# Attention with a routed expert layer on one core: pair numbers of four blocks in their own tiles, later batches' loads and clears between fetches, last stores on SyncE's queue

## The chip, the cores and the metric

The kernel runs on one core of a Trainium2 chip. The metric is the device time of one execution in microseconds (us); the median of several runs counts. The engines are named as the profile names them: PE is the matrix engine, PEld its weight loads, DVE, ACT and POOL the vector, scalar and GpSimd engines, SP the engine whose queue issues most DMAs. Each engine works its instructions off in the order in which they were emitted.

## The reference, cut to what matters

```python
a = einsum('rd,bhsd->bhsr', S1, x); b = einsum('rd,bhsd->bhsr', S2, x)
phi(x) = einsum('bhsi,bhsj->bhsij', a, b).reshape(..., r * r)        # r = 8: 64 features
num = phi(q) @ (phi(k)^T v);  den = phi(q) @ sum_s phi(k) + 1e-06    # per batch and head
x = (num / den) -> (4352, 128)                                       # B=4, H=4, S=1088, head_dim 32
noisy = x @ w_gate + log1p(exp(x @ w_noise)) * noise                 # 8 experts
top2, weights = the two largest of noisy, softmax over the two
out[n] = sum over n's two experts e of weight * (relu(x[n] @ w1[e]) @ w2[e])   # 128 -> 1024 -> 128
```

Everything is fp32. In one sentence: a linear attention over 4 batches makes 4352 token rows of 128, each row goes to two of eight experts (a two-layer network with 1024 hidden units), and the two results are added.

## The kernel before, in words

The four batches' attention and the experts' blocks are interleaved in one instruction stream. The program is not written out by hand: class `Plan` (from L38) collects jobs (`add`), each with the engines that may do it, an estimated cost, what it reads and writes, a priority and the tiles it opens. `order()` then plays the jobs through a simple model of the engines, and of those that could start first (within 0.3 us) takes the one with the lowest priority number. The emitted order on each engine is the planned one, so what the model believes of a transfer's landing decides where the work that needs it is put. A job's `margin` is added to its believed landing. All transfers go through `dma` (L338 is the issuing line), which takes the queue's engine, the priority and the margin. `later(u, ...)` marks loads that are held until the fetch of block u has been issued ("rows u").

The stages, with their lines:

- **Loads.** `load_kq` brings k or q of one batch (544 KB) into a tile `kq` (two buffers), `load_v` brings v in six transfers into `vld` (one buffer), `load_w` brings w1 and w2 of one expert (512 KB each). `clear` writes zeros from the tile `pad` over rows of the DRAM buffer `xs` (516 KB each) ahead of its use.
- **Attention of a batch.** `keys_values`: DVE transposes k and q into kT and qT (L588, L590), PE multiplies them with S1 and S2 (L606), ACT or DVE copies, DVE forms the 64 features per head (L614, L628: `phk`, `phq`), PE sums keys times values (L669) and folds in the gates (L690). `queries`: PE transposes the features (L717), multiplies (L728), DVE divides (L743 to L747, L735).
- **Router.** `router`: a chain of DVE steps (L842 to L999) with counts on PE (L934, L937). It weighs the rows (`xg`, L986), and POOL scatters them by indirect DMAs to `xs` in DRAM (L809, 18 per batch, a spacer memset at L808 before each). A row in `xs` has 129 words: the 128 values and the pair number, which says where its result belongs.
- **Blocks.** Rows of one expert are taken in blocks u = 0 to 47, block u being expert u mod 8 of wave u div 8. Wave 0 holds the first four tiles of batch 0, wave 1 the rest of batch 0, waves 2, 3 and 4 batches 1, 2 and 3; the sixth wave holds what is left over. Blocks of waves 2 to 4 have 256 rows, the others 128. Blocks 0 to 3 are gathered on PE. Blocks 4 to 7 (below `QUICK`) are fetched on POOL's queue, whole rows with their pair numbers, into a tile `xb`, and PE transposes them (L1070). From block 8 on, SP issues four small fetches per block into `xb` (32 KB each) and one for the pair numbers into a tile `ix`, and DVE transposes (`bT`, L1084). `xb` has five buffers and `ix` five. Then come `hp` (L1094, PE), relu (L1102, ACT or L1100, DVE), `acc` (L1109, PE), the copy `y` (L322), and POOL's scatter of the results to the DRAM buffer `pairs` (L809), which reads the pair numbers: out of `xb` for blocks 4 to 7, out of `ix` from block 8 on. The last two blocks (46 and 47) are turned to tokens by a matmul instead (L1241).
- **Sums.** `sums` loads the two results of each token (`pr`), adds them on DVE (L1165; at the end also the matmul's part, L1172) and stores them. The three stores of the very last call are issued on the queues ("ACT", "POOL", "ACT"): 128 rows, 64 rows, 128 rows. Then every engine reads a flag (L1422), a branch follows (L1424) that is not taken unless an expert overflows, and the end barrier (L1452).

What sets the order around the change: SP's queue is one list. Fetches have the priorities −10 + u; k, q and v of batches 2 and 3 have 80 + 100 b and more and wait for "rows 8" and "rows 16". Of the rows of `xs`, clears 4 to 8 wait for the fetches of block 4 to 7 (`DIRECT`) with priorities 64 to 68. An instruction on SP that has to wait for a free buffer holds back all that stands behind it.

Of the kernel before, what the change touches and what calls it, by code (L numbers as in the profile page):

```python
# [174 lines left out]
def kernel(  # L175
# [15 lines left out]
    P = nc.NUM_PARTITIONS  # L191
    B, H, S, DH = q.shape
    R = S1.shape[0]
    D = H * DH
# [38 lines left out]
    def add(engines, cost, emit, **kw):  # L233

        if hold and engines in ("DVE", "PE"):
            kw["after"] = tuple(kw.get("after", ())) + tuple(hold)
        elif hold and engines == EV:
            engines = "ACT"
        return plan.add(engines, cost, emit, **kw)
# [3 lines left out]
    def tag(name, bufs, shape, dtype=F32, space=pool):  # L243
        plan.tag(name, bufs, lambda: space.tile(list(shape), dtype, name=name, tag=name, bufs=bufs))
# [34 lines left out]
    tag("mk", 1, [P, C + 1, E], BF16)  # L279
    tag("lim", 1, [P, E])  # L280
    tag("xb", 5, [P, 2, XW])
    tag("ix", 5, [P, 2])
    tag("bT", 3, [P, 2 * P])
    tag("h", 4, [P, 512])
    tag("y", 10, [P, 2 * D])
# [7 lines left out]
    def vec(n):  # L293
        return 0.155 + 0.00104 * n
# [13 lines left out]
    TABLE = 1.28  # L308
    ROWS = 1.0
    KLATE, VLATE, QLATE = 1.6, 1.3, 1.8  # L310
    MARGIN = 3.0
    LAND = 2.2
    def either(n):
        return {"ACT": act(n), "DVE": vec(n)}
# [715 lines left out]
    def block(u, w, e, r, n):  # L1030

        p0 = 1000 + 100 * u
        bT = new("bT")
        if u < QUICK:
            turn = new("turn")
        if u < DIRECT:
            oh = new("o")
            for c in range(4):
                add(("POOL" if u == 0 and c == 3 else "DVE"), 0.85 if u == 0 and c == 3 else vec(64), lambda e_, c=c: (
                    G if e_ == "POOL" else V).tensor_scalar(  # L1040
                    out=oh.t[:, c, :], in0=place[:], scalar1=onehot["pos"].t[:, c, e:e + 1],
                    scalar2=onehot["gm"].t[:, c, e:e + 1], op0=ALU.is_equal, op1=ALU.mult),
                    r=["place", onehot["pos"], onehot["gm"]], w=[(oh, c)], prio=-900 if u == 0 else 12.5 + u)

            for c in range(4):
                gather = add("PE", mm(P), lambda _, c=c: T.matmul(  # L1046
                    turn.t[:, 0:P], lhsT=onehot["x"].t[:, c, :], rhs=oh.t[:, c, :], start=(c == 0), stop=(c == 3)),
                    lat=0.15, r=[(oh, c), onehot["x"]], w=[turn], prio=p0 - 88)
            while behind_first:
                behind_first.pop().deps.add(gather)  # L1050
            xb = ix = first_rows
        else:
            xb, ix = new("xb"), new("ix")

            def done(ins):
                for w2 in range(w + 1, NW):
                    apart(ins, "scatter%d" % w2)
                behind(ins, *("scatter%d" % w2 for w2 in (w - 1, w)))
                wrote(ins, "fetch", "rows %d" % (u if u >= QUICK else DIRECT))
            there = routed.get(w, []) + routed.get(w - 1, [])  # L1060
            rows = xs_e[e, r:r + P * n, :]
            if u < QUICK:
                fetch = dma("POOL", lambda: xb.t[:, 0:n, :], lambda: rows.rearrange("(c p) x -> p c x", p=P),
                            there, [xb], -10 + u, size=66e3 * n, issue=0.55, done=done)
                for job in held[DIRECT]:
                    job.deps.add(fetch)

                def turns(_):
                    for c in range(n):
                        T.transpose(turn.t[:, P * c:P * c + P], xb.t[:, c, 0:D], ident[:])  # L1070
                add("PE", n * 0.14, turns, lat=0.15, r=[xb, "ident"], w=[turn], prio=p0 - 88)
            else:

                def flat():
                    return xb.t[:].rearrange("p c x -> p (c x)")[:, 0:P * n]
                for l in range(4):
                    fetch = dma("SP", lambda l=l: flat()[32 * l:32 * l + 32, :].rearrange("p (g x) -> p g x", x=32),
                        lambda l=l: rows[:, 32 * l:32 * l + 32].rearrange("(g p) x -> p g x", p=32),
                        there, [(xb, l)], -10 + u, size=16e3 * n, issue=0.5, done=done)
                    for job in held.get(u, ()):  # L1080
                        job.deps.add(fetch)
                dma("SP", lambda: ix.t[:, 0:n].unsqueeze(2), lambda: rows[:, D:XW].rearrange("(c p) x -> p c x", p=P),
                    there, [ix], -10 + u, size=0, issue=0.5, done=done)
                add("DVE", vec(P * n), lambda _: V.transpose(bT.t[:, 0:P * n], flat()), r=[xb], w=[bT], prio=TOP + u)  # L1084
        if u < QUICK:
            add(EV, either(P * n), lambda en: copy(en, bT.t[:, 0:P * n], turn.t[:, 0:P * n]), r=[turn], w=[bT], prio=TOP + u)
        acc = new("acc")
        js = 4 // n
        for g in range(FJ // js):
            hp, h = new("hp"), new("h")  # L1090

            def first(_, g=g, hp=hp):
                for i in range(js):
                    T.matmul(hp.t[:, P * n * i:P * n * (i + 1)], lhsT=w1s[:, e, P * (js * g + i):P * (js * g + i + 1)],  # L1094
                             rhs=bT.t[:, 0:P * n], start=True, stop=True)
            add("PE", js * mm(P * n), first, lat=0.15, r=[bT, ("w1", e)], w=[hp], prio=p0 + 10 * g)

            def relu(en, hp=hp, h=h):
                if en == "DVE":
                    paces.append(V.tensor_scalar_max(h.t[:], hp.t[:], 0.0))  # L1100
                else:
                    paces.append(A.activation(out=h.t[:], in_=hp.t[:], func=AF.Relu))  # L1102
            add(EV, either(512), relu, r=[hp], w=[h], prio=TOP + u)

            def second(_, g=g, h=h):
                for i in range(js):
                    for c in range(n):
                        j = js * g + i
                        T.matmul(acc.t[:, D * c:D * c + D], lhsT=h.t[:, P * (n * i + c):P * (n * i + c + 1)],  # L1109
                                 rhs=w2s[:, e, j, :], start=(j == 0 and c == 0), stop=(j == FJ - 1), skip_group_check=True)  # L1110
            add("PE", 4 * mm(D), second, lat=0.15, r=[h, ("w2", e)], w=[acc], prio=p0 + 10 * g + 15)
        y = new("y")
        add(EV, either(D * n), lambda en: copy(en, y.t[:, 0:D * n], acc.t[:, 0:D * n]), r=[acc], w=[y], prio=TOP + u)
        if w == NW and e >= E - LAST:
            to_tokens(e, ix, y, p0 + 98)
            return
        for c in range(n):
            def emit(_, c=c):
                at = first_at[:, e:e + 1] if u < DIRECT else xb.t[:, c, D:XW] if u < QUICK else ix.t[:, c:c + 1]
                ins = pool_scatter("result", out=pairs[:], in_=y.t[:, D * c:D * c + D], in_offset=None,  # L1120
                                   out_offset=bass.IndirectOffsetOnAxis(ap=at.bitcast(U32), axis=0),
                                   bounds_check=PAIRS - 1, oob_is_err=False)
                apart(ins, "result", "read")
                (behind if w >= NW - 1 else apart)(ins, "zero")
                wrote(ins, "result", "result%d" % w)
            key = ("result", (u, c))
            gone = add("POOL", ROWS + 0.3, emit, r=[y, xb if u < QUICK else ix] + (["zeroed"] if w >= NW - 1 else []),
                       w=[key], prio=400 + 0.01 * u, lat=LAND)
            gone.paced, gone.far = 1.6, True
            results.setdefault(w, []).append(key)  # L1130
# [232 lines left out]
    load_v(1, 49.5)  # L1363
    load_kq(1, "q", 49.6)
    later(DIRECT, lambda: load_w(E - 2, 53), lambda: load_w(E - 1, 54))
    for r in range(4 * P, STATIC, P):
        later(DIRECT, lambda r=r: clear(r, 60 + r / P))
    x, lg, last = queries(0, 0, 4, 10)
    picked = router(0, 0, 4, 0, x, lg, 12)
# [5 lines left out]
    router(0, 4, C + 1 - 4, 1, x, lg, 30)  # L1375
    for b in range(1, B):
        if b > 1:
            later(8 * b - 8, lambda: load_kq(b, "k", 80 + 100 * b), lambda: load_kq(b, "q", 81 + 100 * b), lambda: load_v(b, 82 + 100 * b))
            keys_values(b, 100 * b)
        x, lg, last = queries(b, 0, C + 1, 100 * b + 10)  # L1380
        picked = router(b, 0, C + 1, b + 1, x, lg, 100 * b + 20)
        hold.clear()
        if b == 2:
            zero_pairs(350, [picked])
# [11 lines left out]
        if w == 4:  # L1396
            sums(B - 1, part_of(B - 1, [(0, 4)]), w, 901)
    pieces = part_of(B - 1, [(4, 2), (6, 2)], True)
    sums(B - 1, [pieces[0], pieces[2], pieces[1]], NW, 902, ("ACT", "POOL", "ACT"))

    def idle(a, b):

# [54 lines left out]
```

## Time and profile before

| what | value |
|---|---|
| median of 3 runs | 353.58 us (353.15 to 354.06) |
| the profiled execution, device time | 354.19 us |
| its span | 352.4 us (1.79 us lie around it) |
| granted PE clock, mean | 0.996 |
| PE busy | 337.6 us, 96% of the span |
| DVE, ACT, POOL busy | 146.6, 132.3, 233.8 us |
| moved by DMA | 41.16 MB, 117 GB/s |

The span runs from the first instruction to the last of one execution, and all times in the profile count from its start. PE's busy time is the sum of its matmuls; what is left of the span is PE's idle time. For each group of instructions the profile names what ended the idle time before it (`[0.99 <-DVE row L965]`: 0.99 us idle, ended by DVE's writing of the tile `row` at L965). A wait that was for several things is put down to the one that came last. For a DMA, the issue (SPq, ACTq, POOL) and the landing are two different times; the chain of waits shows the landing as "DMA".

### The profile page before, as it was taken

What the parts mean: (1) busy time and instruction counts of PE and PEld (TensorE: products, weight loads), DVE (VectorE), ACT (ScalarE), POOL (GpSimd) and SP (SyncE); (2) the same over time, 40 slices, a digit from 0 to 9 for tenths busy, and PEclk for the clock granted to TensorE, in tenths of its full rate; (3) what the DMA queues carried; (4) which work ended last, traced back from release to release, by engine and by line L of the source; (5) the groups of instructions that cost most, each with busy time, mean ns of one, the idle gap of its engine ahead of it and who ended that gap; (6) DMA issues with size and microseconds to landing.
All of it is one profiled execution on the core that took longest, in us unless ns stands there. A gap on an engine that the chain in (4) does not pass through costs nothing.

```text
span 352.4 us, 7473 instructions
## 1 busy us (share of the span) xinstructions
PE 337.6 (96%) x2585; PEld 314.5 (89%) x2586; DVE 146.6 (42%) x550; ACT 132.3 (38%) x297; POOL 233.8 (66%) x386
## 2 busy tenths in 40 slices
PE   8999999898999999899999999999999999999992
PEld 3858999898899999789999999999999999999991
DVE  6889885684943675293766000102011000001401
ACT  2343541442442333341343433343334333434330
POOL 8857668882998876879866888887633543354510
PEclk9999999999999999999999999999999999999998
DMA  7999839654411244911432311355315311114521
GB/s 208 347 341 219 301 89 316 243 174 87 79 43 47 54 78 76 287 53 31 81 63 48 64 50 39 67 149 147 69 31 146 106 32 24 30 31 139 162 80 37
DMA packets 68297, 41.16 MB, mean 117 GB/s; under 512 B 49301, under 2 KB 60438, under 8 KB 68256
## 3 DMA queue, kind: packets, MB, share of 16 engines
q1 hardware_dynamic: 62784, 30.92, 34.6%
q0 software_dynamic: 4736, 9.19, 7.9%
q10 hardware_dynamic: 736, 0.54, 0.6%
q8 instruction: 21, 0.34, 0.4%
q14 instruction: 20, 0.16, 0.2%
HBM read 24.17 MB, written 16.65 MB: 116 GB/s over the span
## 4 chain that ended last, share of the span: by engine, by line
PE 88%; DVE 3%; SPq 2%; DMA 2%; issue 1%; ACT 1%; POOL 0%; DVEq 0%; POOLq 0%; ACTq 0%
PE hp L1094 34%; PE acc L1109 34%; PE bank L606 5%; PE bank L728 4%; PE bank L669 4%; PE bank L717 2%; SPq L338 2%; DMA kq<-in_k_dram 1%; PE hp L1417 1%; PE acc L669 1%; PE turn L1046 1%; PE bank L1241 1%; DVE xg L986 1%; DMA xb<-xs 1%; PE bank L690 0%
## 5 line engine op out<-in xcount | busy, mean ns | idle before, releaser
L1109 PEld LDWEIGHTS acc<-w2s,h 128*128 128x128 f32 x1152 | 146.3, 192 | 5.2 <-issue 0.2
L1109 PE MATMUL acc<-w2s,h 128*128 128x128 f32 x1152 | 150.7, 275 | 0.0
L1094 PE MATMUL hp<-bT,w1s 128*128 128x128 f32 (+1 forms) x768 | 148.5, 329 | 1.7 <-DVE row L965 1.0
L1102 ACT ACTIVATE h<-hp 128x512 f32<-128x512 f32 x143 | 85.4, 597 | 130.2 <-PE hp L1094 111.8
L1094 PEld LDWEIGHTS hp<-bT,w1s 128*128 128x128 f32 x768 | 111.6, 191 | 7.9 <-issue 1.5
L809 POOL DMA_INDIRECT pairs<-y,ix x62 | 61.1, 986 | 58.8 <-ACT y L322 48.8
L809 POOL DMA_INDIRECT xs<-xg,to x72 | 74.3, 1032 | 26.6 <-DVE xg L986 12.8
L1084 DVE STREAM_TRANSPOSE bT<-xb 128x256 f32<-128x256 f32 (+1 forms) x40 | 15.6, 389 | 119.1 <-PE hp L1094 92.6
L808 POOL MEMSET zb<- 128x400 bf16 (+1 forms) x142 | 63.2, 445 | 0.2
L322 ACT COPY y<-acc 128x128 f32<-128x128 f32 (+1 forms) x48 | 15.3, 319 | 23.1 <-PE acc L1109 18.5
L728 PE MATMUL bank<-kvw,pT 128*128 128x98 f32 x144 | 18.2, 274 | 0.1
L1165 DVE TENSOR_TENSOR o<-pr 128x512 f32<-128x512 f32 (+2 forms) x13 | 6.7, 519 | 27.7 <-DMA pr<-pairs 27.6
L728 PEld LDWEIGHTS bank<-kvw,pT 128*128 128x128 f32 x144 | 17.3, 192 | 0.6 <-DVE kvw L322 0.3
L322 ACT COPY pT<-bank 128x512 f32<-128x512 f32 (+1 forms) x17 | 9.2, 549 | 12.3 <-PE bank L717 6.1
L669 PE MATMUL bank<-phk,vaug 128*128 128x128 f32 (+1 forms) x108 | 13.1, 277 | 0.0
L669 PEld LDWEIGHTS bank<-phk,vaug 128*128 128x128 f32 (+1 forms) x108 | 12.6, 191 | 0.4
L628 DVE TENSOR_TENSOR phk<-ab 128x512 f32<-128x512 f32 (+1 forms) x20 | 12.2, 629 | 0.4
L322 ACT COPY lo<-bank 128x256 f32<-128x256 f32 (+3 forms) x20 | 6.2, 326 | 16.2 <-PE bank L606 8.4
L628 DVE TENSOR_TENSOR phq<-ab 128x512 f32<-128x512 f32 (+1 forms) x20 | 12.0, 632 | 0.3
L717 PE MATMUL bank<-ident,phq 128*128 128x128 f32 x72 | 10.8, 277 | 1.1 <-ACT kvw L322 1.1
L606 PE MATMUL bank<-sk,kT 128*128 128x128 f32 (+1 forms) x64 | 9.2, 286 | 2.5 <-DVE kT L590 1.6
L606 PEld LDWEIGHTS bank<-sk,kT 128*128 128x128 f32 (+1 forms) x64 | 7.5, 184 | 4.3 <-DVE kT L590 2.3
(178 smaller groups left out, 245.4 us busy)
## 6 DMA issues: line engine op xcount, KB each, us to landing
xs<-pad SPq DMA_DIRECT2D x9, 516.0 KB
w1s<-in_moe_w_dram SPq DMA_DIRECT2D x8, 512.0 KB
w2s<-in_moe_w_dram SPq DMA_DIRECT2D x8, 512.0 KB
pr<-pairs SPq DMA_DIRECT2D x7, 512.0 KB
xb<-xs SPq DMA_DIRECT2D x96, 32.0 KB
kq<-in_k_dram SPq DMA_DIRECT2D x4, 544.0 KB
kq<-in_q_dram SPq DMA_DIRECT2D x4, 544.0 KB
vld<-in_v_dram SPq DMA_DIRECT2D x14, 128.0 KB
```

The source lines that it names most:

```text
L322: paces.append(A.copy(o, i) if e == "ACT" else V.tensor_copy(o, i))
L606: T.matmul(ps.t[rows, 2 * W * i:2 * W * i + 2 * W], lhsT=lhsT, rhs=sk[:].rearrange("p c h x -> p (c h x)"), start=True, stop=True)
L628: V.tensor_tensor(out=jobs[i][2].t[rows, jobs[i][1]:jobs[m - 1][1] + 1, :, :].rearrange("p c h (i j) -> p (c h) i j", i=R), in0=factors(i, ...
L669: T.matmul(kvp.t[:, P * a:P * a + P], lhsT=va.t[0:K, t, hs, :].rearrange("p h d -> p (h d)"), rhs=pk.t[0:K, t, hs, :].rearrange("p h f -> ...
L717: T.transpose(ps.t[:, c0:c0 + P], pq.t[:, t + i, 2 * a:2 * a + 2, :].rearrange("p h f -> p (h f)"), ident[:])
L728: T.matmul(ps2.t[:, c0:c0 + 2 * YW], lhsT=pT.t[:, P * (2 * i + a):P * (2 * i + a) + P], rhs=kvw.t[:, a, :], start=True, stop=True)
L808: G.memset(zb[:, 0:FIRST_SPACER if kind == "first" else SPACER], 0.0)
L809: ins = G.indirect_dma_start(**kw)
L1084: add("DVE", vec(P * n), lambda _: V.transpose(bT.t[:, 0:P * n], flat()), r=[xb], w=[bT], prio=TOP + u)
L1094: T.matmul(hp.t[:, P * n * i:P * n * (i + 1)], lhsT=w1s[:, e, P * (js * g + i):P * (js * g + i + 1)], rhs=bT.t[:, 0:P * n], start=True, st ...
L1102: paces.append(A.activation(out=h.t[:], in_=hp.t[:], func=AF.Relu))
L1109: T.matmul(acc.t[:, D * c:D * c + D], lhsT=h.t[:, P * (n * i + c):P * (n * i + c + 1)], rhs=w2s[:, e, j, :], start=(j == 0 and c == 0), st ...
```

## The change

It has five parts. (1) Blocks 4 to 7 get their pair numbers by an own small fetch on SP's queue into `ix`, which now has ten buffers; their result scatters read `ix` like all others. Their `xb` is still fetched whole on POOL's queue. (2) The planner believes the k, q and v loads of batches 2 and 3 to land later (`MARGIN` 3 to 6) and the block fetches on SP 1.0 later. (3) The last three clears (`6 * P` to `8 * P`) move from behind blocks 4 to 7 to a place between the fetches of blocks 14 and 15. (4) k, v and q of batches 2 and 3 get priorities between those of fetches: k behind block 9 or 17, v behind 10 or 18, q behind 12 or 20. (5) The last two stores go to SP's queue.

```diff
@@ tags and planner
-    tag("ix", 5, [P, 2])
+    tag("ix", 10, [P, 2])
-    MARGIN = 3.0
+    MARGIN = 6.0
@@ block(u, w, e, r, n), fetches of u >= QUICK
                         lambda l=l: rows[:, 32 * l:32 * l + 32].rearrange("(g p) x -> p g x", p=32),
-                        there, [(xb, l)], -10 + u, size=16e3 * n, issue=0.5, done=done)
+                        there, [(xb, l)], -10 + u, size=16e3 * n, issue=0.5, done=done, margin=1.0)
                     for job in held.get(u, ()):
                         job.deps.add(fetch)
-                dma("SP", lambda: ix.t[:, 0:n].unsqueeze(2), lambda: rows[:, D:XW].rearrange("(c p) x -> p c x", p=P),
-                    there, [ix], -10 + u, size=0, issue=0.5, done=done)
                 add("DVE", vec(P * n), lambda _: V.transpose(bT.t[:, 0:P * n], flat()), r=[xb], w=[bT], prio=TOP + u)
+            dma("SP", lambda: ix.t[:, 0:n].unsqueeze(2), lambda: rows[:, D:XW].rearrange("(c p) x -> p c x", p=P),
+                there, [ix], -10 + u + (0.5 if u < QUICK else 0), size=0, issue=0.5, done=done)
@@ the result scatter
-                at = first_at[:, e:e + 1] if u < DIRECT else xb.t[:, c, D:XW] if u < QUICK else ix.t[:, c:c + 1]
+                at = first_at[:, e:e + 1] if u < DIRECT else ix.t[:, c:c + 1]
...
-            gone = add("POOL", ROWS + 0.3, emit, r=[y, xb if u < QUICK else ix] + (["zeroed"] if w >= NW - 1 else []),
+            gone = add("POOL", ROWS + 0.3, emit, r=[y, ix] + (["zeroed"] if w >= NW - 1 else []),
@@ the main body
-    for r in range(4 * P, STATIC, P):
+    for r in (4 * P, 5 * P):
         later(DIRECT, lambda r=r: clear(r, 60 + r / P))
...
     for b in range(1, B):
         if b > 1:
-            later(8 * b - 8, lambda: load_kq(b, "k", 80 + 100 * b), lambda: load_kq(b, "q", 81 + 100 * b), lambda: load_v(b, 82 + 100 * b))
+            early = 8 * b - 16.5
+            later(8 * b - 8, lambda: load_kq(b, "k", early), lambda: load_v(b, early + 1), lambda: load_kq(b, "q", early + 3))
+            if b == 2:
+                for r in range(6 * P, STATIC, P):
+                    later(8, lambda r=r: clear(r, early + 5))
             keys_values(b, 100 * b)
...
-    sums(B - 1, [pieces[0], pieces[2], pieces[1]], NW, 902, ("ACT", "POOL", "ACT"))
+    sums(B - 1, [pieces[0], pieces[2], pieces[1]], NW, 902, ("ACT", "SP", "SP"))
```

## The prediction, as put on record

> **What bounds the kernel now.** I read the busy line of the page, then the busy time by stretches, then the gaps on TensorE, then for each gap the engine and the queue behind it, and the end last. The page, sections 1 and 2:
>
> ```profile
> span 352.4 us, 7473 instructions
> PE 337.6 (96%) x2585; PEld 314.5 (89%) x2586; DVE 146.6 (42%) x550; ACT 132.3 (38%) x297; POOL 233.8 (66%) x386
> PE   8999999898999999899999999999999999999992
> ```
>
> TensorE (PE) is busy 337.6 of 352.4 us, so only 14.8 us can be gained without taking work from it. Its digits dip in few slices, at the end most. In stretches of 10 us (columns: stretch, length, busy time with count of PE, PEld, DVE, ACT, POOL, clock, DMA share, GB/s):
>
> ```profile
> 70.00:80.00 10.00, 10.00 (x99) 9.99 (x98) 7.33 (x51) 4.50 (x12) 8.46 (x15) 1.00 0.58 166
> 80.00:90.00 10.00, 8.19 (x72) 7.84 (x70) 5.97 (x19) 3.18 (x7) 3.92 (x5) 1.00 0.40 85
> 140.00:150.00 10.00, 8.65 (x63) 8.07 (x62) 2.44 (x6) 3.13 (x6) 8.53 (x12) 1.00 0.94 271
> 150.00:160.00 10.00, 9.31 (x69) 8.36 (x68) 8.82 (x18) 4.26 (x12) 7.95 (x11) 1.00 0.15 44
> 200.00:210.00 10.00, 10.00 (x69) 9.38 (x68) 0.45 (x1) 3.83 (x8) 9.01 (x13) 1.00 0.22 53
> ```
>
> From about 160 to 340 us PE is full (10.00 of 10.00). What idles in the middle lies in 80 to 90 (1.81 us), 140 to 150 (1.35) and 150 to 160 (0.69). The timeline of PE names them; the bracket is the idle time before the entry:
>
> ```profile
> 83.58 1.13 PE L1094 MATMUL hp<-bT,w1s 128*128 128x128 f32 x8 [0.99 <-DVE row L965]
> 90.02 2.05 PE L606 MATMUL bank<-sk,kT 128*128 128x128 f32 x16 [0.84 <-DVE lim L998]
> 148.33 2.05 PE L606 MATMUL bank<-sk,kT 128*128 128x128 f32 x16 [1.35 <-DVE kT L590]
> 156.31 1.13 PE L1094 MATMUL hp<-bT,w1s 128*128 128x256 f32 x4 [0.69 <-ACT h L1102]
> ```
>
> They sum to 0.99 + 0.84 + 1.35 + 0.69 = 3.87 us. (One more, 1.05 us at 63.19, waits for ACT's copies at L322, whose order the change leaves alone; it stays.) The first comes from a fetch that DVE waited 3.88 us for, and that was issued at 78.84 although its rows had long been in DRAM (timelines of SP, DVE and POOL):
>
> ```profile
> 74.86 0.43 SPq L338 DMA_DIRECT2D kq<-in_q_dram  x1
> 78.84 4.19 SPq L338 DMA_DIRECT2D xb<-xs  x7
> 83.12 0.31 DVE L1084 STREAM_TRANSPOSE bT<-xb 128x128 f32<-128x128 f32 x1 [3.88 <-DMA xb<-xs]
> 74.30 0.97 POOL L809 DMA_INDIRECT pairs<-y,xb  x1 [0.17 <-issue]
> 87.44 1.40 POOL L809 DMA_INDIRECT xs<-xg,to  x1 [4.51 <-DVE xg L986]
> ```
>
> SP stood still between 75.8 and 78.84: block 9 needs one of the five xb buffers, and the one due belonged to block 4, whose result scatter (POOL, 74.30) still reads its pair numbers out of xb; it landed at 78.15. DVE, which works in order, then stood in front of the router's rest: POOL's scatters of the next rows started 4.51 us late, and DVE reached batch 2's kT transposes late, at 89.26 (the 0.84 gap). The third gap is in the chain of waits; the load that it hangs on was queued behind all fetches of its wave:
>
> ```profile
> 142.49 5.04 DMA kq<-in_k_dram
> 147.56 0.72 DVE kT L590
> 148.33 3.58 PE bank L606 x28
> ```
>
> At the end, the last matmul ends at 345.73 and the three last stores are issued from 345.22 on. The end barrier:
>
> ```profile
> L1452 POOLq DRAIN  x3: 109/193/3422, 347.7 to 352.0; - x3
> L1452 SPq DRAIN  x3: 7/7/13, 350.4 to 351.4; - x3
> ```
>
> POOL's first DRAIN starts at 347.67 and lasts 3.42 us, to 351.09; SP, which waits for all stores to land (the last at 349.06), reaches its own at 350.43. POOL is last by 0.66 us, and 1.3 us of barrier follow.
>
> **What the skill says.** The Trainium skill, "DMA: Bandwidth & Descriptors", section "Anatomy of one DMA — SWDGE (gpsimd) path": the DMA engines don't wait on semaphores; a wait is served on the issuing sequencer. The trace agrees: SP's 3.0 us held seven fetch transfers back. The same section puts the fixed cost of a DMA at about 2.0 us; the small fetches here land 1.5 to 2.1 us after issue (2.7 to 3.5 beside big loads). Its section "Issuing engines are not separate DMA queues": another issuer saves only sequencer time. The last stores agree: landing 2.78 us after issue from ACT, 2.45 from POOL. "Perfetto Trace Analysis", section "Sequencer-only Instruction (DRAIN, etc)": the recorded time of a DRAIN is its execution, without the wait before it; so I read the 3.42 us as POOL's own work.
>
> **The change, part by part.** The baseline is the profiled execution, 354.19 us (span 352.4 and 1.79 around it); the median shown, 353.58, is 0.61 less. The instructions of PE are the same in number; building the changed kernel shows their order the same up to block 8, batch 2's features one group earlier, batch 3's about 14 groups earlier, and the same again from about 184 us on.
>
> 1. Pair numbers. Four DMAs more on SP (about 0.45 us of issue each, 1.8 in all), queued before the weights of experts 6 and 7. They wait for the same routing as POOL's fetches (landed at 49.74), and w1s of expert 6 was issued at 49.89, needed at 72.1: cost 0 to 0.5 us there, hidden by 15 us and more; uncovered it would be 1.8. Block 4's xb is free once PE has transposed it (L1070, first at 48.6) and not at 78.15. Block 9's fetch then goes behind block 8's, about 72.4 to 74.3, and lands near 76; DVE wants it at about 79.3 (83.12 less its 3.88). First gap: −0.99. DVE's two waits, 3.88 and 0.59, go, so that it is through the router by about 85.5 where PE wants kT near 87: second gap −0.84. POOL's scatters start near 83 where it was 87.44.
>
> 2. k, v, q of batches 2 and 3 between fetches. Batch 2's k is issued at about 74.8 (it was 74.49) and lands 3.7 us later, wanted at 85.5: nothing lost. But its DMAs now stand before fetches: v is six issues at about 0.45, 2.7 us before block 11's fetch, which then lands near 84.5 (wanted 91.7, so 7 us of cover). Batch 3's k is issued after the fetches of blocks 16 and 17. The scatters that these wait for ended at 115.35 and now at about 111; fetches 113.5 to 118.2; k at about 118.4, landing 3.7 to 5.0 us later, 122 to 123.5. Third gap: −1.35, and the fourth (ACT's relu behind DVE's crowded 8.82 of 10 us) goes with the place it stood in: −0.69, the least sure of the four. But in the changed order kT is transposed in the middle of batch 2's router on DVE, which got there at 130.5 and will at about 128.5: 5 us of slack. Beyond it PE, DVE and POOL all wait.
>
> 3. Three clears of 516 KB between the fetches of blocks 14 and 15: issue some 1.3 us each, so block 15 lands near 97 to 99, wanted by DVE near 101: 0, at worst 1.5. The same clears are gone from 52 to 60 us, where weights and scatters ran beside them: gain 0 to 0.5; taken 0, since PE's gaps there aren't theirs.
>
> 4. The planner's margins (3 to 6, and 1 on fetches) add no instruction; they only choose the order above. What the new interleaving costs in new small waits no row shows. The kind is there: PE waits 0.3 to 1.1 us where ACT or DVE stands in order behind something else. Bounds 0 to 2.0; taken 0.3.
>
> 5. Last stores on SP. POOL has no DMA left at the end, so its DRAIN should come early: −0.66 until SP's own arrival is last. SP issues the last store at 346.22 at the earliest (0.6 us against ACT's 1.03), so it lands 0.1 to 0.4 sooner; a load of the flag (0.73 us on SP) now comes after it, beside the landing. Taken −0.8; bounds +0.3 (SP's queue serial) and −1.3.
>
> Sum: −3.87 + 0.3 − 0.8 = −4.4, so 354.19 − 4.4 = 349.8 profiled, 349.2 as a median. PE's full stretch from 160 to 340 only shifts.
>
> **The rivals.**
> A. As worked out, 349.2. For it: each gap has a named cause that the change removes. Chance 0.50.
> B. The middle gains half: PE waits anew where batch 3's features, with up to 8.82 us of DVE per 10, fall beside batch 2's router (7.39 and 5.92 in 120 to 140). 8.82 + 5.92 passes 10 by 4.7 in the worst case, half of it hidden by PE's other queued work, as I assume: +2.3, so 351.5. Against it: the products come after the router in the new order. Chance 0.24.
> C. The end gains nothing (POOL's DRAIN takes 3.42 us wherever it stands, and waits for the others): 350.0. Chance 0.15.
> D. Slower: batch 3's k lands late. It costs one for one beyond 5 us of slack and passes the gain of 4.4 only when it lands after 128.5 + 4.4 = 132.9, 14.5 us after its issue; PE and DVE then stand in order. Two 544 KB loads, six v loads and fetches together could do that; the slowest such load so far (q of batch 2) took 6.95. At 17 us it loses 118.4 + 17 − 128.5 = 6.9 against 4.4 gained: 349.2 + 6.9 = 356.1. Chance 0.11, other mishaps of that size within it.
>
> **How the numbers follow.** About 0.3% (1 us) is what a measurement here can tell from no change. A, C and nearly all of B (0.82 of the 0.89) are faster; the worst end of B and the mild half of D, 0.08, fall within 1 us; 0.10 is slower. The range runs from every unknown at its best (354.19 − 3.87 − 0.5 − 1.3, less 0.61: 347.9) to new waits of 2.0 with the tail at its worst (354.19 − 3.87 + 2.0 + 0.3, less 0.61: 352.0); D and the worst end of B stay outside.
>
> **What would show it.** Right: no gap over 0.5 us on PE between 80 and 160; block 9's fetch issued before 75; the first scatter after it near 83; no 3.4 us DRAIN of POOL after the last matmul, and the end within 6 us of it (now 6.67). Wrong: a PE gap at L606 with kT behind a load of k; DVE waiting for xb near 92 to 102; PE gaps at L669 or L728 behind DVE; SP's DRAIN later than 350.4 less the shift.

## The result and the profile after

The changed kernel takes 350.51 us in the median (349.27 to 353.08, 18 runs), the kernel before 353.62 in the same runs; the ratio is 0.9922, 95% interval 0.9901 to 0.9943, so 2.8 us less (2.0 to 3.5). In a second set of runs, beside other experiments, it was 0.9930 (0.9903 to 0.9957). The forecast was 4.4 less. The profiled execution took 352.57 us with a span of 350.6; before it was 354.19 and 352.4. Around the span lie 2.0 to 2.1 us in all 18 runs, where it was 1.79 in the profiled execution before, so some 0.3 us of the change fall outside what the profile shows. The page after, sections 1 and 2:

```profile
span 350.6 us, 7490 instructions
PE 337.2 (96%) x2586; PEld 314.1 (90%) x2586; DVE 147.5 (42%) x550; ACT 132.9 (38%) x297; POOL 234.3 (67%) x385
PE   8999999998999999999999999999999999999991
```

PE's work is the same (337.2 of busy time against 337.6). The dips in the middle are nearly gone. In stretches of 10 us, with the columns as before:

```profile
70.00:80.00 10.00, 8.55 (x75) 8.18 (x74) 6.81 (x48) 3.94 (x10) 8.77 (x15) 1.00 0.43 109
80.00:90.00 10.00, 9.91 (x95) 9.82 (x95) 7.11 (x22) 3.56 (x8) 6.07 (x9) 1.00 0.53 117
140.00:150.00 10.00, 10.00 (x74) 9.16 (x73) 6.21 (x14) 3.69 (x8) 9.01 (x13) 1.00 0.44 113
150.00:160.00 10.00, 10.00 (x88) 9.43 (x88) 5.89 (x17) 2.27 (x5) 9.01 (x14) 1.00 0.13 41
```

The four gaps of before are not there: 80 to 90 idles 0.09 (was 1.81), 140 to 160 nothing (was 2.04). But 70 to 80 idles 1.45, where it was 0. The timeline of PE after, all gaps over 0.3 us between 40 and 340:

```profile
80.08 0.19 PE L934 MATMUL bank<-mk,earlier 128*128 128x72 bf16 x1 [1.34 <-DVE mk L927]
131.72 0.19 PE L934 MATMUL bank<-mk,earlier 128*128 128x72 bf16 x1 [0.32 <-DVE mk L927]
132.46 2.05 PE L606 MATMUL bank<-sk,kT 128*128 128x128 f32 x16 [0.33 <-DVE kT L590]
```

The steps that the prediction named can be read off the timelines of SP and POOL after: block 9's fetch is issued at 72.87 (was 78.84) and the scatters of wave 2 start at 85.27 (was 87.44; 83 was forecast).

```profile
72.87 1.82 SPq L338 DMA_DIRECT2D xb<-xs  x4
85.27 1.40 POOL L809 DMA_INDIRECT xs<-xg,to  x1 [1.65 <-DVE xg L986]
```

Three of the prediction's signs of being right are not met: those scatters are not near 83, a gap of 1.34 us ends at 80.08 (none over 0.5 was to be left from 80 to 160), and the end is not within 6 us of the last matmul. That matmul ends at 343.06, 2.67 us earlier than before (345.73). Yet the span ends only 1.8 us earlier: from the last matmul to the end it is now 7.5 us, where it was 6.67. First the line of the flag's read on SP (durations in ns, then the start):

```profile
L1426 SPq TENSOR_LOAD <-flag x1: 979/979/979, 344.6 to 344.6; - x1
```

Then SP's branch and the waits that stand behind it (durations, first and last start):

```profile
L1428 SPq EVENT_SEMAPHORE  x8: 17/17/17, 348.1 to 348.7; - x8
...
L1428 SPq COMPARE_BRANCH  x1: 45/45/45, 345.6 to 345.6; - x1
```

The end barrier:

```profile
L1456 POOLq DRAIN  x3: 46/103/3341, 335.6 to 350.1; - x3
L1456 SPq DRAIN  x3: 7/7/13, 349.5 to 349.8; - x3
```

And of the waits of SP's queue (us in total, times, longest) the one behind the branch, which names no other engine or transfer:

```profile
SPq L1428 <- SPq L1428: 2.5, 1, 2.5
```

POOL's long DRAIN (an engine's own instruction before the end barrier) has gone to 335.6, as forecast. SP now ends last: its last store is issued at 343.55 (0.98 us), then comes the flag's load (0.98), the branch at 345.63, and its next instruction only at 348.14, although the last store has landed by 346.48. Twenty short wait instructions (1.34 us) lead to its DRAIN at 349.5, and 1.06 us of barrier follow.

### The profile page after: what moved, and what is told of

It is laid out like the page before. It is cut to its first block, busy times and chain, and to the rows that moved or that the text cites. A ratio compares the mean times of both kernels' runs of the same rounds, so it can differ in the third digit from the quotient of the medians.

```text
span 350.6 us, 7490 instructions
## 1 busy us (share of the span) xinstructions
PE 337.2 (96%) x2586; PEld 314.1 (90%) x2586; DVE 147.5 (42%) x550; ACT 132.9 (38%) x297; POOL 234.3 (67%) x385
## 4 chain that ended last, share of the span: by engine, by line
PE 84%; DVE 5%; DMA 4%; POOL 2%; issue 1%; SPq 1%; ACT 1%; POOLq 0%; DVEq 0%
PE acc L1109 34%; PE hp L1094 33%; PE bank L606 4%; PE bank L728 4%; PE bank L669 4%; DMA kq<-in_k_dram 2%; PE bank L717 2%; POOL pairs L809 1%; DMA xb<-xs 1%; PE turn L1046 1%; PE bank L1241 1%; SPq L338 1%; DVE kT L590 1%; POOL zb L808 0%; DMA ix<-xs 0%
## 5 line engine op out<-in xcount | busy, mean ns | idle before, releaser
L1094 PE MATMUL hp<-bT,w1s 128*128 128x128 f32 (+1 forms) x768 | 148.2, 328 | 0.2 <-ACT h L1102 0.2
L1094 PEld LDWEIGHTS hp<-bT,w1s 128*128 128x128 f32 x768 | 111.7, 191 | 6.2 <-ACT h L1102 0.7
L809 POOL DMA_INDIRECT pairs<-y,ix x66 | 65.8, 997 | 64.2 <-ACT y L322 52.8
L809 POOL DMA_INDIRECT xs<-xg,to x72 | 74.3, 1031 | 20.2 <-issue 9.6
L614 DVE TENSOR_TENSOR ab<-bank,lo 128x256 f32<-128x256 f32 (+3 forms) x20 | 7.2, 361 | 12.3 <-ACT lo L322 12.0
L986 DVE TENSOR_TENSOR xg<-x,g 128x512 f32<-128x512 f32 (+1 forms) x16 | 11.2, 748 | 0.0
L1421 PE MATMUL hp<-zb 128*128 128x512 bf16 x30 | 9.3, 442 | 1.7 <-DVE zb L439 1.3
```

Of the source, the lines that this page charges most:

```text
L809: ins = G.indirect_dma_start(**kw)
L986: V.tensor_tensor(out=xg.t[:, i, c0:c1, 0:D], in0=x.t[:, c0:c1, :], in1=B_["g"].t[:, i, c0:c1].unsqueeze(2).to_broadcast([P, c1 - c0, D]), ...
```

## The experiments

Ratios are to the kernel before in the same set of runs, with 95% intervals; 0.001 is 0.35 us.

| kernel | ratio | last matmul to end | PE idle from 22 us to its last matmul |
|---|---|---|---|
| before | 1 | 6.67 | 6.5 (1.06 of it at 63 us) |
| the change | 0.9922 (0.9901 to 0.9943) | 7.5 | 4.1 |
| the change, second time | 0.9930 (0.9903 to 0.9957) | 7.4 | 2.7 |
| change, stores all on ACT | 0.9884 (0.9864 to 0.9904) | 5.9 | 2.1 |
| change, stores as before | 0.9895 (0.9852 to 0.9938) | 6.7 | 2.4 |
| before + stores on SP | 1.0052 (1.0027 to 1.0076) | 7.5 | 4.9 |
| before + clears moved | 1.0138 (1.0090 to 1.0186) | 6.5 | 9.8 |
| before + pair numbers | 0.9906 (0.9870 to 0.9942) | 6.5 | 2.5 |
| before + loads and margins | 0.9873 (0.9830 to 0.9916) | 6.7 | 3.6 |
| before + margins | 0.9890 (0.9851 to 0.9930) | 6.7 | 2.5 |
| before + pair numbers, stores on ACT | 0.9890 (0.9858 to 0.9922) | 5.2 | 3.5 |
| change, k and v later, stores on ACT | 0.9857 (0.9815 to 0.9899) | 5.6 | 4.1 |
| change without the branch | 0.9795 (0.9752 to 0.9838) | 3.6 | 3.8 |
| change, clears back | 0.9897 (0.9859 to 0.9936) | 7.8 | 2.9 |

The last two columns come from one profiled execution each (idle time summed over the trace's matmuls).

### The end: who is last

**All three last stores on ACT.**

```diff
-    sums(B - 1, [pieces[0], pieces[2], pieces[1]], NW, 902, ("ACT", "SP", "SP"))
+    sums(B - 1, [pieces[0], pieces[2], pieces[1]], NW, 902, ("ACT", "ACT", "ACT"))
```

> The changed kernel, with all three last stores on ACT's queue (none on SP or POOL). Theory S (SP's own list ends last in the changed kernel: last store's issue 0.98, flag load 0.98, branch, 2.5 us until its next instruction, then 20 short waits): SP now has its branch behind it long before the last store lands, so the end hangs on the landing: from the last matmul some 3.4 us to the landing, 1.4 of SP's waits and 1.1 of barrier, 5.9 us where the changed kernel has 7.5; the time falls by about 1.6, to 348.9. Rival L (the end hangs on the stores' landing in the changed kernel as well, and the queue makes no difference): no change, 350.5.

Measured: 349.06 us, ratio 0.9884, and 5.9 us from the last matmul to the end. Theory S holds; the other two runs with all stores on ACT end 5.2 and 5.6 us after the last matmul. SP's branch and the waits behind it in this run:

```profile
L1428 SPq EVENT_SEMAPHORE  x8: 17/17/17, 338.8 to 344.3; - x8
...
L1428 SPq COMPARE_BRANCH  x1: 45/45/45, 336.1 to 336.1; - x1
```

Its end barrier:

```profile
L1456 SPq DRAIN  x3: 7/7/13, 345.1 to 345.4; - x3
```

The branch is at 336.1, and 2.7 us pass here too before SP's next instruction (338.8), but nobody waits for them: the last matmul ends at 340.3. SP is held by the landing of the last store (344.20) and reaches its DRAIN 0.9 us after it; in the changed kernel that took 3.0.

**The last stores as before, on the changed kernel.** The edit restores ("ACT", "POOL", "ACT").

> The changed kernel with its last stores as before (ACT, POOL, ACT); all else changed. Theory S: POOL's DRAIN ends last again, 6.7 us from the last matmul to the end instead of 7.5: 0.8 faster than the changed kernel, 349.7. The view of the prediction (moving the stores gains 0.8): 0.8 slower, 351.3.

Measured: 349.76 us, ratio 0.9895, end 6.7 us after the last matmul, POOL's DRAIN last again (from 342.66, 3.42 us). This goes with theory S, though the two intervals overlap (0.9852 to 0.9938 here, 0.9901 to 0.9943 for the change).

**The stores on SP, on the kernel before.** The edit is the change's last line alone.

> The kernel before with nothing changed but the last two stores on SP's queue. Theory S: 0.8 slower than before, 354.4, with a pause of about 2.5 us behind SP's branch. The view of the prediction: 0.8 faster, 352.8. The order of all instructions up to the end is that of the kernel before, so the gap of PE at 63 us tells something too: if it belongs to the order or to the traffic of the clears it is there again (1.05 us), if it is an accident of one execution it may be gone.

Measured: 355.28 us, ratio 1.0052, clear of no change: this part by itself costs 1.8 us (1.0 to 2.7). The trace shows 0.8 of them in the span (7.47 against 6.67 from the last matmul), with 2.6 us behind SP's branch. Some 0.65 more lie between span and device time: 2.3 to 2.5 us in all 22 runs, 1.7 to 1.9 in the 41 of the kernel before; what they are the trace does not show. And the gap at 63 us is gone. PE's timeline of this run, with the gaps that remain:

```profile
62.11 0.60 PE L717 MATMUL bank<-ident,phq 128*128 128x128 f32 x4
...
82.23 1.13 PE L1094 MATMUL hp<-bT,w1s 128*128 128x128 f32 x8 [0.88 <-DVE row L965]
88.53 2.05 PE L606 MATMUL bank<-sk,kT 128*128 128x128 f32 x16 [0.71 <-issue]
...
148.60 1.16 PE L606 MATMUL bank<-sk,qT 128*128 128x128 f32 x8 [0.85 <-issue]
154.74 1.13 PE L1094 MATMUL hp<-bT,w1s 128*128 128x256 f32 x4 [0.69 <-ACT h L1102]
```

The same order of instructions has no bracket at L717: the 1.05 us of before were not the order's, but an accident of one execution. The other four gaps are there with 0.88 + 0.71 + 0.85 + 0.69 = 3.13 us, for 3.87 in the profile of before.

**Without flag and branch.** The edit takes out the `values_load` of the flag and `with tc.If(outer != 0): outside()`.

> The changed kernel (last stores on ACT, SP, SP) without the read of the flag and without the branch and the program behind it; it leaves out the case in which an expert gets more rows than it has room for, which these inputs don't reach. Theory S: behind its last store SP has neither the flag load (0.98) nor the 2.5 us after the branch, so the end hangs on the landing: 5.9 us from the last matmul to the end where the changed kernel has 7.5, 348.9 us. Rival L (the end hangs on the stores on SP's queue): as the changed kernel, 350.5.

Measured: 347.35 us, ratio 0.9795, and 3.6 us from the last matmul (342.76) to the end; 5.9 was expected. SP's waits and its DRAIN, with nothing between them and the last store's issue at 343.25:

```profile
L1452 SPq EVENT_SEMAPHORE  x11: 17/28/28, 343.9 to 346.3; - x11
...
L1452 SPq DRAIN  x3: 7/7/7, 345.5 to 345.8; - x3
```

The direction is theory S's, the size is larger: the last store lands at 345.36, and the span ends 0.97 us later, since SP's other waits are passed while that store is under way. So flag, branch and what queues behind them cost the changed kernel 3.9 us of its 7.5 in the traces (the two ratios differ by 0.0127, 4.5 us). How the 3.9 divide between the flag's load, the branch and the waits was not tried. It is a measurement, no version to use: it leaves out the case of an overfull expert.

### The middle: one root or four

**Pair numbers alone.**

```diff
-    tag("ix", 5, [P, 2])
+    tag("ix", 10, [P, 2])
-                at = first_at[:, e:e + 1] if u < DIRECT else xb.t[:, c, D:XW] if u < QUICK else ix.t[:, c:c + 1]
+                at = first_at[:, e:e + 1] if u < DIRECT else ix.t[:, c:c + 1]
...
```

> The kernel before with only the pair numbers of blocks 4 to 7 in their own tiles. Theory M (the middle's gain needs the pair numbers and the loads together): block 9's fetch no longer waits for block 4's scatter, so PE's gap at about 82 (0.88 in the run with only the tail changed) is gone; but k, q and v of batch 2 keep the lowest rank and now come out behind all fetches up to block 15, so kT is late: a new gap at L606 of 1 to 5 us near 90 to 100, and batch 3's gap (0.85 to 1.35) stays. Net slower than before, 354 to 357. Rival P (the pair numbers alone bring the first two gaps' gain): 352.0, 1.6 under before.

Measured: 350.51 us, ratio 0.9906: theory M falls. Batch 2's k is indeed issued late (89.32), and DVE waits 2.22 us for it, but PE doesn't: the planner knew, and put blocks before its features, which stand 80 matmuls later in PE's order than before. So this run does not separate the freed buffer from the new order that comes with it. The stretches of this run:

```profile
80.00:90.00 10.00, 10.00 (x92) 10.00 (x91) 5.28 (x17) 3.70 (x8) 7.21 (x10) 1.00 0.33 54
140.00:150.00 10.00, 10.00 (x76) 9.27 (x75) 7.03 (x15) 4.67 (x14) 9.03 (x12) 1.00 0.57 166
150.00:160.00 10.00, 9.31 (x76) 8.29 (x75) 5.52 (x11) 2.27 (x5) 8.74 (x14) 1.00 0.14 44
```

The gap of batch 3's k is gone too, though k stands behind its whole wave as before. With block 9's fetch on time the scatters of wave 2 are issued from 83.5 to 111.3 (86.0 to 113.9 in the run with only the tail changed), the fetches follow, k is issued at 136.6 instead of 140.2, and lands at 141.85; PE comes to it at 143.58. Its first matmul on kT is the 1150th in both kernels, so here it is the earlier k that counts. The fourth gap stays, with the same 0.69 us:

```profile
151.62 1.13 PE L1094 MATMUL hp<-bT,w1s 128*128 128x256 f32 x4 [0.69 <-ACT h L1102]
150.97 0.60 ACT L1102 ACTIVATE h<-hp 128x512 f32<-128x512 f32 x1 [1.00 <-PE hp L1094]
```

ACT's relu waits for PE's `hp` here and PE then for the relu, with DVE busy 5.52 of 10 us where it was 8.82 before.

**Loads between fetches, and margins.** The edit is parts 2 and 4 of the change, with the clears, the pair numbers and the stores as before.

> The kernel before with only the k, v, q loads of batches 2 and 3 placed between fetches, and the planner's margins. Theory M: block 9's fetch still waits for the scatter of block 4, so the gap near 82 and what follows it stay (about 1.6 us); batch 3's k no longer comes behind its wave, so the gaps near 148 and 156 (0.85 to 1.35, and 0.69) go: 1.5 to 2.0 gained, 351.7. Rival (the gaps only move): no gain within 0.5.

Measured: 350.04 us, ratio 0.9873, 4.5 us less (3.0 to 6.0), more than expected. Block 9's fetch still waits for block 4's scatter and is issued at 79.85, but the wait for it on DVE is 0.98 us and not 3.88. The four gaps are gone, and the profile has two others, 0.93 us at L1094 (77.57) and 1.11 at L934 (80.74). Something other than the queue had helped, so the margins were tried apart.

**Margins alone.**

```diff
-    MARGIN = 3.0
+    MARGIN = 6.0
-                        there, [(xb, l)], -10 + u, size=16e3 * n, issue=0.5, done=done)
+                        there, [(xb, l)], -10 + u, size=16e3 * n, issue=0.5, done=done, margin=1.0)
```

> The kernel before with only the planner's margins changed (6 for later batches' loads, 1 for fetches); no instruction is added, and SP's loads stay in their places. Theory O (order): the planner puts DVE's transpose of block 9 behind the router's next three steps and PE's features of batch 3 later, so the same late fetches are waited for less: PE's gaps near 82, 88, 148 and 156 (3.1 us together in the run with only the tail changed) shrink by half or more; 1.5 to 3 us gained, 351. Theory Q (queue: only moving what stands in SP's list helps): gaps as before, 353.5.

Measured: 349.67 us, ratio 0.9890. Theory O holds, with 3.9 us gained (2.5 to 5.3): two numbers in the planner, without an instruction added, bring as much as the whole change of the middle, within the intervals. SP's list stays nearly that of before (one piece of v, for instance, goes from in front of block 9's fetch to behind block 11's). Its stretches:

```profile
80.00:90.00 10.00, 9.78 (x86) 9.54 (x85) 8.03 (x22) 3.72 (x9) 7.45 (x10) 1.00 0.45 95
140.00:150.00 10.00, 10.00 (x75) 9.46 (x74) 4.52 (x10) 4.42 (x10) 8.75 (x13) 1.00 0.86 223
```

DVE's timeline around block 9's transpose:

```profile
79.33 0.23 DVE L967 SCALAR_TENSOR_TENSOR row<-c,row 128x72 f32<-128x72 f32 x1
80.95 0.31 DVE L1084 STREAM_TRANSPOSE bT<-xb 128x128 f32<-128x128 f32 x1 [1.39 <-DMA xb<-xs]
```

The fetch comes no earlier relative to what surrounds it (issued at 76.94, behind k and q), but DVE does three router steps first and then waits 1.39 us. And batch 3's k, issued at 139.33 and landed at 144.58, is used by PE at 147.03: its features stand later in the order, so nothing waits.

**Pair numbers and stores on ACT, no load moved.**

> The kernel before with the pair numbers of blocks 4 to 7 in their own tiles and the last stores all on ACT; no load, clear or margin moved. Theory R (one root: block 4's buffer; the moved loads add nothing on top of it): as the changed kernel with the stores on ACT, ratio to before 0.988, about 349.3. Rival (the moved loads are worth a us of their own): 350.3 or more.

Measured: 350.02 us, ratio 0.9890, beside 0.9884 for the whole change with the stores on ACT. Theory R holds within the intervals (0.9858 to 0.9922): the moved loads and margins add nothing that can be seen on top of the pair numbers, though 1 us either way would be hidden in these intervals. This run's profile has the fourth gap again (0.69 us, at 154.34) and one of 1.14 us at L606, behind DVE's transpose of batch 2's q, which like k is loaded behind all fetches up to block 15 here.

### The clears, k, and the order's own spread

**Clears moved alone.** The edit is part 3, with the clears at rank 4.5, the middle's other parts as before.

> The kernel before with only the last three clears moved between the fetches of blocks 14 and 15 (the planner then also moves other instructions of the middle). If the clears' traffic between 52 and 66 us made PE's gap at 63: that gap is gone, and up to 1.05 us are gained, unless PE then waits at the router's counts (L934) near 80 as in the changed kernel; the wait of DVE for block 9's fetch (3.88) stays, since block 4's buffer is still held by its scatter. If the gap was an accident or the order's: it is there, and the time is that of before within 0.5.

Measured: 358.39 us, ratio 1.0138, 4.9 us more. The planner spread the clears over the fetches and put batch 2's k behind them; SP's timeline:

```profile
74.26 1.19 SPq L338 DMA_DIRECT2D xs<-pad  x2
79.72 3.66 SPq L338 DMA_DIRECT2D xb<-xs  x8
83.42 0.55 SPq L338 DMA_DIRECT2D xs<-pad  x1
84.09 3.10 SPq L338 DMA_DIRECT2D xb<-xs  x4
87.23 0.43 SPq L338 DMA_DIRECT2D kq<-in_k_dram  x1
```

k at 87.23 (73.31 with only the tail changed) gives PE gaps of 1.32, 2.57 and 0.60 at L606 between 92 and 98, and 1.98 at 152. Part of the difference goes with PE's clock: this profile, at 360.93 us the slowest of the six runs, has 0.984 granted and PE busy 341.4 us, that of before 0.996 and 337.6. No gap at 63 us.

**Clears back, on the changed kernel.**

> The changed kernel with the last three clears back behind the weights (52 to 66 us) where the kernel before has them. By the prediction's reckoning the move costs and brings nothing: the time of the changed kernel within 0.5. If the clears' traffic early made PE's gap at 63 us: that gap is back, 1 us slower. If they hold up block 15's fetch now (issued at 97.7, landed at 104.2 in the changed kernel): faster by up to 1.

Measured: 350.82 us, ratio 0.9897 (0.9859 to 0.9936), not to be told from the change. The clears run at their old time and there is no gap at 63 us, as in the run with only the tail changed: their traffic alone does not make it.

**k and v one fetch later, stores on ACT.**

```diff
-            later(8 * b - 8, lambda: load_kq(b, "k", early), lambda: load_v(b, early + 1), lambda: load_kq(b, "q", early + 3))
+            later(8 * b - 8, lambda: load_kq(b, "k", early + 1), lambda: load_v(b, early + 2), lambda: load_kq(b, "q", early + 3))
```

> The changed kernel with the last stores all on ACT, and k and v of batches 2 and 3 one fetch later (k behind the fetches of blocks 10 and 18). In the changed kernel DVE waits 1.8 us for block 10's rows and 2.2 for block 18's, which are fetched beside k. Theory K (that wait made PE's gaps at L934, 1.34 and 0.32, and at L606, 0.33, in the profile of the changed kernel): DVE's waits shrink to under 1 us and those gaps don't appear; the median falls by 0 to 1.0 below the run with three stores on ACT (349.1), since that run had none of these gaps in its profiled execution. Rival: k then lands too late, a gap at L606, slower by 0.5 or more.

Measured: 349.4 us, ratio 0.9857 (0.9815 to 0.9899), beside 0.9884 (0.9864 to 0.9904) with k in its place: inconclusive. The profile contradicts theory K: DVE waits 2.55 us for a block's rows before kT at 87, and PE has 0.64 at L934, 1.28 at L606 and 0.68 at L717.

**The changed kernel a second time.**

> The changed kernel again, for a second profiled execution and for a time beside the others of this call. If PE's gaps at 80 (1.34 at L934) and 132 (0.65) are a matter of how transfers fall in one execution: other sizes this time, in sum anything from 0 to 2.5 us. If they belong to the order: the same again. The end from the last matmul: 7.5 us again. Time 350.5.

Measured: 350.93 us. PE waits 0.65 us at L934 near 79 and 0.33 at L606 near 131, where it was 1.34, 0.32 and 0.33; with the stores on ACT or as before, the same order of the middle shows none and 0.66 at L934, and without the branch 1.04 at L606 near 87, 0.33 at L934 and 0.33 at L606 near 132. So one order has 0 to 2.0 us of these waits, as transfers and semaphores fall in one execution. The end is 7.4 us.

## Why the prediction was right, and where it was not

**The first and second gap (−0.99, −0.84): right.** Block 9's fetch went out at 72.87, within the forecast 72.4 to 74.3, and both gaps are gone. The pair numbers alone do it, the new order that they bring included. The scatters that follow started at 85.27, not at 83: DVE waited 1.80 us for block 10's rows, issued from 76.94 on behind k, whose own issue took 1.54 us. In the four other executions of the same order they started between 83.4 and 84.8, with DVE idle for 1.5 to 2.9 us ahead of block 10's transpose. The prediction counted what v delays, and put nothing for the fetch right behind k: in the three executions that show all of its landings, block 10's pieces landed 3.0 to 5.9 us after issue. (The section from which the prediction quotes a fixed cost of about 2.0 us gives it for DMAs that GpSimd issues. These fetches are issued on SP, and the times measured here, 1.5 to 2.1 us and more beside big loads, are the ones that count.)

**The third gap (−1.35): right in size, one cause too narrow.** The prediction gave it to k's new place. It goes without that, by the pair numbers alone and by the margins alone. It was a later effect of the first root: DVE, in order, stood in front of a transpose whose rows came late, POOL's scatters started late, and the fetches and k behind them. So by these runs three of the four gaps hang on one root, with more than one remedy, and the remedies don't add: 0.9906, 0.9873 and 0.9890 singly, 0.9895 together. That moving loads without changing margins would help by itself was not tried. Part 4, of which the prediction said "they only choose the order", was undervalued: by itself it brings 3.9 us.

**The fourth gap (−0.69): right, but not for DVE's sake.** It goes with the place that it stood in, as forecast. It stands with 0.69 us in all four profiles that keep this piece of the order (before, with only the tail changed, and twice with the pair numbers alone in the middle), whatever the transfers did, and in none with the new margins. That ACT's relu came late because DVE was crowded is not borne out: with DVE busy 5.52 of 10 us it is the same, and the relu waits for PE (0.99 us before, 1.00 with the pair numbers alone).

**New waits (+0.3): undersized in the profile of after.** That shows 1.34 + 0.32 + 0.33 and two of 0.2, 2.4 us, while the 1.05 us at 63 that the prediction let stay are absent. In the four other executions of this order the new waits are 0 to 1.7 us. The middle as a whole is right: −3.87 + 0.3 = −3.6 forecast, 3.7 measured for the change with its stores as before (2.2 to 5.2). There is some luck in how close that is: in the second profile of the old order the four gaps sum to 3.13 and not 3.87.

**Block 15 and batch 3's k: covered, as said.** Block 15 landed at 104.5 and not at 97 to 99, without a gap on PE over 0.25 us; k was issued at 121.85 and landed at 125.84 (118.4 and 122 to 123.5 forecast), before DVE came to it at 131.7. Rival D did not happen.

**The end: this step failed.** "Taken −0.8; bounds +0.3 (SP's queue serial) and −1.3." It is +0.8 in the trace, and 1.8 (1.0 to 2.7) in time where it stands alone. Its sign was wrong. What failed is the clause that the flag's load comes "beside the landing". POOL's DRAIN did leave the end, but behind SP's last store stand the issue (0.98, not 0.6), the flag's load (0.98, not 0.73), 2.5 us after the branch, and twenty waits that can begin only then. In the kernel before, SP had its branch behind it at 341.5 and then waited for a landing at 348.0, which covered all of that:

```profile
L1424 SPq EVENT_SEMAPHORE  x8: 17/17/17, 348.0 to 349.6; - x8
...
L1424 SPq COMPARE_BRANCH  x1: 45/45/45, 341.5 to 341.5; - x1
```

No row of that profile could show what stands behind the branch when nothing covers it. The prediction priced the load that it saw and gave the branch behind it, unseen, nothing; a bound for the unknown would have put the high end of this step above +0.3. The 1.6 us between −0.8 and +0.8 make up the miss: 4.4 − 1.6 = 2.8, as measured. The intervals (2.2 to 5.2 for the middle, 2.0 to 3.5 for the whole) leave room for other divisions, and the 0.3 us outside the span belong to it too.

Rival C named the right place (the end gains nothing) for another reason: it had POOL's DRAIN stay.

**A faster version.** With all three stores on ACT the changed kernel takes 349.06 us, below both kernels: its interval (0.9864 to 0.9904) only just touches those of the change (0.9901 to 0.9943 and 0.9903 to 0.9957).

## What to carry to other kernels

Before an engine is given the last store, list what stands behind that store in its own queue (flag reads, branches, waits before the barrier): work that was covered by a landing becomes the end. When several gaps have late DMAs behind them, look for the first one in time and remove that alone; the others may be its echoes, as two of three were here. And where a planner orders the work, its belief about when data lands can be worth as much as the transfer (3.9 us here by two numbers): an in-order engine loses by standing too early in front of a tile.

## What was not expected of the hardware

SP's next instruction came 2.5 to 2.9 us after its branch in the nine traces in which no landing covers it (2.51 in the changed kernel, 2.94 in that with pair numbers alone), while ACT, DVE and POOL took 0.2 to 0.6. In each of the 13 traces with the branch a transfer of 8 KB on the queue that the page calls "instruction" (q14) starts 0.9 to 1.4 us after it (in the changed kernel at 346.56, and another at 345.62, as the branch starts); the run without the branch has none in its last 20 us. That they are what SP waits for is not shown.

In the traces with the branch, POOL's first DRAIN at the end takes 3.34 us where POOL's last DMA was a result scatter and 3.42 where it was a store. It starts 1.7 to 2.0 us after that DMA was issued in each of them, so it is early where POOL's last DMA is early. It does not wait for the landing: with the pair numbers alone POOL's store landed at 343.32, and the DRAIN lasted to 346.40. This agrees with the Trainium skill, "Perfetto Trace Analysis", section "Sequencer-only Instruction (DRAIN, etc)": the record is execution, and the wait for semaphores is not in it. In the run without the branch it lasts 4.56 us, and there the record does take in other work: it begins before POOL's own last scatter and ends 3.4 us after it.

```profile
L1452 POOLq DRAIN  x3: 45/102/4562, 333.3 to 346.1; - x3
333.56 0.98 POOL L809 DMA_INDIRECT pairs<-y,ix  x1 [2.15 <-ACT y L322]
```

The statement in "DMA: Bandwidth & Descriptors", section "Issuing engines are not separate DMA queues", that another issuer saves only the sequencer's time, usually small beside the transfer, needs a caution from this case: at the end the sequencer decided. The stores landed 2.1 to 3.0 us after issue from either queue, but what stood behind the issue was worth 1.6 us between SP and ACT (7.5 against 5.9 us).
